# A recurrent layer's third chunk: its sa by tokens is transposed from saT instead of computed as a product of its own

## The chip, the cores and the metric

The kernel runs on one core of a Trainium2 chip. The metric is device time in microseconds of one execution. Before the change three runs took 644.02, 644.89 and 645.16 us, a median of 644.89 us.

## What is computed

A recurrent attention block (RWKV-7 style) feeds a feed-forward block with an exact GELU. All arrays are float32 in the recurrence; batch 4, 8 heads, 768 tokens, head dimension 40. For the feed-forward block the 3072 tokens have 320 features each, and 2048 hidden units.

```python
for t in range(S):
    y[:, :, t] = np.einsum('bhd,bhde->bhe', rt, state)
    Sa = np.einsum('bhde,bhe->bhd', state, at)
    state_decay = state * wt[:, :, None, :] - np.einsum('bhd,bhe->bhde', Sa, bt)
    state = state_decay + np.einsum('bhd,bhe->bhde', vt, kt)
...
x = np.ascontiguousarray(attn_out.transpose(0, 2, 1, 3)).reshape(B * S, H * D)
h = x @ w_in
g = 0.5 * h * (1.0 + erf(h * inv_sqrt2))
return (g @ w_out).astype(np.float32)
```

## The kernel before

**Chunks.** The 768 tokens are cut into 12 chunks of 64 (c = 0 to 11). Within a chunk the recurrence is turned into matrix products: masked token-by-token matrices N, A, M and RV, the inverse of a triangular matrix (Tt, built by an elimination on GpSimd), and the products that give the chunk's outputs and the state for the next chunk. Four batches times eight heads make 32 small problems, which sit two by two on the partition halves of TensorE, so that one such product is 32 matmuls of 64x64 or 64x40. A float32 matmul is shown in the trace as two matmuls and two weight loads.

**The feed-forward part** of a chunk (`ph`: the first matrix, `gelu`, `po`: the second) is laid between the steps of the recurrence of later chunks, so that TensorE has long products to run while the other engines mask, copy and transpose.

**Order.** Nothing is scheduled by a program: every engine carries out its instructions in the order in which the kernel's functions are called. Chunks 0 to 4 stand written out call by call; from chunk 5 on a loop does it. The change lies in the written-out part, at the end of the third chunk (c = 2, lines 1864 to 1893).

**sa.** For a chunk the vectors Sa of all its tokens are needed in two layouts. `saT` (line 1064) has features on partitions; it enters M = `products(saT, rT)`. `sa` by tokens enters the state tile `SM` next to the masked M, and `make_QY` multiplies `SM` with the scaled b. There are two ways to get the second layout:

- `make_sa` and `copy_sa` (lines 1050 and 1059): a second product of the same two factors as saT with their roles exchanged, 32 matmuls of 64x40 into the PSUM tile `sap`, and one copy of 128x640 by ScalarE into `SM`. Chunks 0 to 2 do this.
- `sa_blocks` (line 1082): `turn_sa` lets VectorE transpose `saT` in 32x32 blocks into a tile `sa` (it takes the place named "nT" in SBUF), and `move_sa` copies 16 blocks to where they belong in `SM`: blocks 0 to 3 by VectorE (32x256), 4 to 7 by ScalarE (32x256), and 8 to 15 by ScalarE (32x64). Chunks 3 and 4 use it; later chunks call the two halves of it apart.

**PSUM places.** PSUM is used as four places of two banks; the table `places` (line 99) says by name and chunk which place a tile gets. A new tile in a place waits until the last reader of the old one is done. In the stretch of the change: M_ps of chunk 2 is in place 2, sap of chunk 2 in place 1, kT_ps of chunk 3 in place 2, the `ph` tile that follows in place 1, A_ps of chunk 3 in place 2.

**Fills.** `keep(n)` asks for a filler matmul of n times 128 columns; the next call of `duo` (line 125), whatever tile that is for, issues it into that tile ahead of the tile's own products.

**Side tiles.** `saT` and the `vT` of the next chunk share one place in SBUF ("late"), so `turn_v(3)` waits until all readers of saT are done. The raw pairs of r of the next chunk are loaded by SyncE (`load_r(4)`) once `turn_r(3)` has read the old ones.

Of the kernel before, what the change touches and what calls it, by code (L numbers as in the profile page):

```python
# [21 lines left out]
def kernel(  # L22
# [72 lines left out]
    def keep(*columns):  # L95

        asked[:] = columns
# [27 lines left out]
    def duo(name, at):  # L125
        pt = psum.tile([P, 2, 512], FP32, tag="duo" + places[name][at], name=name, bufs=1)
        while asked:
            n = asked.pop()
            mm(pt[:, 0, :n * P], ident, cum_m.unsqueeze(1).to_broadcast([P, n, P]))
        return pt  # L130

    def half(j, n=HP):
        return slice(j * HP, j * HP + n)
# [4 lines left out]
    def mm(o, lhsT, rhs, first=True):  # L138
        nc.tensor.matmul(o, lhsT, rhs, start=first, stop=True, skip_group_check=True)  # L139
# [204 lines left out]
    def flat(t):  # L344
        return t.rearrange("p j g n t -> p (j g n) t")
# [333 lines left out]
    def flip_k(c):  # L679
        turned_in[c]["kT_ps"] = flip(by_pair(turned_in[c]["ks"]), "kT_ps", c)  # L680
# [73 lines left out]
    def masked(to, pt):  # L754
        nc.vector.tensor_tensor(to, pt, upper.unsqueeze(1).to_broadcast([P, 2 * G * NP, C]), ALU.mult)
# [12 lines left out]
    def units():  # L768
        for i in range(NP):
            for g in range(G):  # L770
                for x in range(2):
                    for e in range(2):
                        yield g, i, x, e, i // NA, 2 * (i % NA) + x
# [276 lines left out]
    def make_sa(c):  # L1050
        t = turned_in[c]
        xs = t["xs"]
        Tt = t["Tt"]
        sap = t["sap"] = duo("sap", c)[:, :, :G * NP * D].rearrange("p x (g q a d) -> p x g q a d", g=G, q=2, a=NA)
        for g, i, x, e, q, m in units():
            at = (g * NP + i) * D
            mm(sap[half(e), x, g, q, i % NA], Tt[half(e ^ x), x, g, i], xs[half(e ^ x), x, at:at + D])

    def copy_sa(c):
        sap = turned_in[c].pop("sap")  # L1060
        copy = nc.scalar.copy if 0 < c < NS else nc.vector.tensor_copy
        copy(SM.rearrange("p g q (a x) c -> p x (g q a) c", x=2)[:, :, :, :D], sap.rearrange("p x g q a d -> p x (g q a) d"))
# [19 lines left out]
    def sa_blocks(c, blocks):  # L1082

        if "sa" not in turned_in[c]:
            turn_sa(c)
        move_sa(c, blocks)

    def turn_sa(c):
        t = turned_in[c]
        if True:  # L1090
            t["sa"] = side("sa", "nT", 1).rearrange("p g n t -> p (g n) t")
            nc.vector.transpose(t["sa"].rearrange("p n t -> p (n t)"), t["saT"].rearrange("p q m e t -> p (q m e t)"))  # L1092

    def move_sa(c, blocks):
        t = turned_in[c]
        for n in blocks:
            d, g, e, z = n // 8, n // 4 % 2, n // 2 % 2, n % 2
            to, at = e * HP + z * BL, g * HP + d * BL
            end = (BL, D)[d]
            copy = nc.scalar.copy if d or n >= 4 else nc.vector.tensor_copy  # L1100
            copy(SM[to:to + BL, g].rearrange("p q m c -> p (q m) c")[:, :, d * BL:end],  # L1101
                 t["sa"][at:at + BL, :, to:to + end - d * BL])
# [5 lines left out]
    def mask_M(c):  # L1108
        t = turned_in[c]
        masked(flat(SM)[:, :, D:], t.pop("M_ps"))  # L1110
# [316 lines left out]
    def put(c, g):  # L1427
        os = work.tile([P, DM], FP32, tag=f"os{g}", name="os")
        nc.vector.tensor_copy(os, pos[c][:, g])
        for e in range(2):  # L1430
            row = (G * e + g) * S + c * C
            nc.sync.dma_start(out=out[row:row + C], in_=os[half(e)])
# [443 lines left out]
    make_M(2)  # L1876
    put(0, 1)
    mask_M(2)
    keep(2)
    make_sa(2)  # L1880
    copy_sa(2)
    flip_k(3)
    turn_v(3)
    copy_k(3)
# [432 lines left out]
```

## Time and profile before

| | |
|---|---|
| median of three runs | 644.89 us |
| the profiled execution, its time | 643.49 us |
| its span in the profile | 641.8 us |
| TensorE matmuls, busy | 624.2 us, 14788 records |
| TensorE weight loads, busy | 553.9 us, 14788 records |
| VectorE, busy | 450.5 us |
| ScalarE, busy | 373.5 us |
| GpSimd, busy | 392.2 us |

How to read the lines below. Times are microseconds from the span's start. A line of a timeline has the start, the length, the engine (PE is TensorE's matmuls, PEld its weight loads, DVE VectorE, ACT ScalarE, POOL GpSimd, SPq the queue of SyncE), the line of the kernel, the operation, the tile written and the tiles read, the shape and the number of instructions put together; in brackets stands how long the engine had been idle before it and what it waited for. A line of the windows view has the stretch, its length, and for PE, PEld, DVE, ACT and POOL the busy time with the number of instructions in brackets; then TensorE's granted clock, the DMA engines' share and GB/s. A line of the chain has start, length and what ran; "issue" is time in which the engine waited for nothing that the profile shows. A line of a DMA queue has packets, MB and the time of the packets as a share of 16 engines' span.

### The profile page before, as it was taken

How to read it: one execution, taken by the hardware profiler on the slowest of the kernel's cores; microseconds unless marked ns; L12 is line 12 of the kernel's file. 1: busy time of each engine (PE TensorE's matmuls, PEld its weight loads, DVE VectorE, ACT ScalarE, POOL GpSimd, SP SyncE). 2: the span in 40 equal slices, each digit the busy share in tenths (PEclk: the TensorE clock that was granted, in tenths of full speed). 3: DMA queues.
4: the chain of work that ended last, by engine and by line, in shares of the span. 5: the costliest groups of instructions: out<-in, count | busy, mean ns of one | idle time of the engine just before them, and what ended most of it. 6: DMA issues, size and time to landing. Idle time of an engine off the chain costs nothing.

```text
span 641.8 us, 32951 instructions
## 1 busy us (share of the span) xinstructions
PE 624.2 (97%) x14788; PEld 553.9 (86%) x14788; DVE 450.5 (70%) x604; ACT 373.5 (58%) x717; POOL 392.2 (61%) x806
## 2 busy tenths in 40 slices
PE   6899899999999999999999999999999999999997
PEld 4787788787878899998998998988989989989977
DVE  1775889996467899685995995985987965623313
ACT  4437694664265479447487587576587687274020
POOL 7587478822857814898848858858758768620000
PEclk9999899999999999999999999999999999999999
DMA  9986767448234643465555466374465450210100
GB/s 139 176 143 138 131 137 164 104 106 149 60 75 75 117 99 67 94 113 120 111 105 100 95 116 115 74 130 86 80 120 106 84 98 5 43 25 10 35 2 21
DMA packets 227119, 60.47 MB, mean 94 GB/s; under 512 B 208603, under 2 KB 225275, under 8 KB 226978
## 3 DMA queue, kind: packets, MB, share of 16 engines
q1 hardware_dynamic: 225946, 56.33, 47.2%
q8 instruction: 116, 1.90, 1.3%
q0 software_dynamic: 592, 1.70, 1.2%
q10 hardware_dynamic: 440, 0.33, 0.2%
q14 instruction: 25, 0.20, 0.1%
HBM read 50.46 MB, written 3.93 MB: 85 GB/s over the span
## 4 chain that ended last, share of the span: by engine, by line
PE 86%; DVE 4%; POOL 3%; SPq 2%; DMA 2%; ACT 2%; issue 1%; ACTq 0%; DVEq 0%; POOLq 0%
PE ph L1414 33%; PE po L1317 22%; PE QY L139 7%; PE po L1424 5%; PE po L1250 2%; PE J L139 2%; PE N_ps L139 2%; PE RV_ps L139 2%; PE saT_ps L139 2%; PE M_ps L139 2%; POOL st L863 2%; POOL st L861 2%; PE A_ps L139 1%; PE X L139 1%; PE av L139 1%
## 5 line engine op out<-in xcount | busy, mean ns | idle before, releaser
L1414 PE MATMUL ph<-xt,w_in_sb 64*64 64x256 f32 (+1 forms) x3360 | 218.4, 377 | 1.9 <-issue 1.8
L1414 PEld LDWEIGHTS ph<-xt,w_in_sb 64*64 64x64 f32 (+1 forms) x3360 | 175.1, 141 | 30.1 <-DMA v_pairs<-in_v_dram 1.7
L861 POOL TENSOR_TENSOR tmp<-W,Nb 128x126 f32<-128x126 f32 (+22 forms) x310 | 129.5, 418 | 57.6 <-DVE Nb L876 34.1
L863 POOL TENSOR_TENSOR W<-W,tmp 128x126 f32<-128x126 f32 (+22 forms) x310 | 147.3, 475 | 24.3
L1418 ACT ACTIVATE gt<-ph 128x1024 f32<-128x1024 f32 x48 | 49.2, 1025 | 92.4 <-PE ph L1414 89.0
L1317 PE MATMUL po<-w_out_sb,gt 128*128 128x160 f32 x576 | 84.3, 302 | 0.0
L1317 PEld LDWEIGHTS po<-w_out_sb,gt 128*128 128x128 f32 x576 | 79.2, 190 | 1.2
L1218 ACT COPY turned<-within 8x64 f32<-8x64 f32 (+3 forms) x144 | 46.4, 322 | 3.5 <-DVE within L1207 1.6
L814 POOL TENSOR_TENSOR VR<-VR,upper 128x1024 f32<-128x1024 f32 x8 | 18.9, 2366 | 30.2 <-ACT VR L810 26.7
L580 ACT COPY part<-part 32x256 f32<-32x256 f32 (+1 forms) x112 | 36.1, 322 | 1.7
L1424 PE MATMUL po<-w_out_sb,gt 128*128 128x320 f32 x128 | 36.5, 438 | 0.5 <-DVE w_out_sb L386 0.5
L1092 DVE STREAM_TRANSPOSE sa<-saT 128x1024 f32<-128x1024 f32 x9 | 11.1, 1238 | 32.1 <-ACT saT L1079 32.1
L1101 ACT COPY SM<-sa 32x64 f32<-32x64 f32 (+1 forms) x108 | 31.8, 294 | 1.4
L1424 PEld LDWEIGHTS po<-w_out_sb,gt 128*128 128x128 f32 x128 | 23.7, 190 | 10.2 <-DVE w_out_sb L386 1.0
L1340 DVE TENSOR_TENSOR os<-os,po 128x160 f32<-128x160 f32 x63 | 19.7, 314 | 17.4 <-PE po L1317 10.5
L1337 ACT COPY os<-po 128x160 f32<-128x160 f32 x9 | 2.6, 290 | 41.9 <-PE po L1317 41.9
L376 ACT ACTIVATE conv<-conv,rebias 128x320 uint32<-128x320 uint32 (+1 forms) x26 | 15.8, 620 | 15.7 <-DVE conv L373 15.6
L1317 PE MATMUL po<-extra,half 128*128 128x160 f32 x160 | 23.2, 299 | 0.0
L876 DVE STREAM_TRANSPOSE Nb<-N 128x1024 f32<-128x1024 f32 x10 | 21.6, 2158 | 1.7 <-ACT N L798 1.7
L1035 DVE COPY Tt<-J 32x512 f32<-32x512 f32 x9 | 6.2, 689 | 23.2 <-PE J L139 23.2
L1317 PEld LDWEIGHTS po<-extra,half 128*128 128x128 f32 x160 | 22.2, 190 | 0.0
L1317 PE MATMUL po<-extra,gt 128*128 128x160 f32 x144 | 21.1, 300 | 0.0
(301 smaller groups left out, 1280.7 us busy)
## 6 DMA issues: line engine op xcount, KB each, us to landing
VR<-in_v_dram SPq DMA_DIRECT2D x24, 160.0 KB
out_dram<-os SPq DMA_DIRECT2D x45, 80.0 KB
b_rows<-in_b_dram SPq DMA_DIRECT2D x22, 160.0 KB
k_rows<-in_k_dram SPq DMA_DIRECT2D x22, 160.0 KB
a_pairs<-in_a_dram SPq DMA_DIRECT2D x18, 144.0 KB
v_pairs<-in_v_dram SPq DMA_DIRECT2D x36, 72.0 KB
r_pairs<-in_r_dram SPq DMA_DIRECT2D x36, 72.0 KB
a_pairs<-in_b_dram SPq DMA_DIRECT2D x16, 144.0 KB
```

The lines of the kernel that those rows point to most:

```text
L139: nc.tensor.matmul(o, lhsT, rhs, start=first, stop=True, skip_group_check=True)
L580: nc.scalar.copy(to[at:at + BL, :, x, z * BL:end], tmp[on:on + BL, e, :, q * BL:q * BL + end - z * BL])
L861: eng.tensor_tensor(t, W[:, :rows, j:j + 1].to_broadcast([P, rows, rest]), Nb[:, j:j + 1, j + 1:].to_broadcast([P, rows, rest]), ALU.mult)
L863: eng.tensor_tensor(W[:, :rows, j + 1:], W[:, :rows, j + 1:], t, ALU.add)
L876: nc.vector.transpose(Nb.rearrange("p s t -> p t s"), N[:, :, :BL].rearrange("p n t -> p t n").unsqueeze(2).to_broadcast([P, BL, 2, NBL]))
L1101: copy(SM[to:to + BL, g].rearrange("p q m c -> p (q m) c")[:, :, d * BL:end], t["sa"][at:at + BL, :, to:to + end - d * BL])
L1218: nc.scalar.copy(tn[to:to + deep, :, at:at + wide], within[0][at:at + deep, :, to:to + wide])
L1317: nc.tensor.matmul(self.pt[at][:, n, :DM // 2], l_[:, f], r_[:, f], start=f == 0, stop=f == NF // 2 - 1)
L1340: nc.vector.tensor_tensor(to, one_, other, ALU.add)
L1414: nc.tensor.matmul(pt[to:end, x, s], w_in_sb[half(x), kt, p * P + to:p * P + end], xt[half(x), kt], start=kt == 0, stop=kt == NK - 1)
L1418: nc.scalar.activation(gt[:, 4 * q:4 * q + 4].rearrange("p (x s) t -> p x s t", x=2), phs.pop((c, q)), ACT.Gelu)
L1424: nc.tensor.matmul(pos[c][:, g], gt[:, f, g * P:(g + 1) * P], w_out_sb[:, f], start=f == 0, stop=f == NF - 1)
```

## The change

In the third chunk `sa` by tokens is taken from saT: `sa_blocks(2, ...)` takes the place of `make_sa(2)` and `copy_sa(2)`.

```diff
     make_M(2)
     put(0, 1)
     mask_M(2)
+    sa_blocks(2, range(0, 8))
     keep(2)
-    make_sa(2)
-    copy_sa(2)
+    sa_blocks(2, range(8, 16))
     flip_k(3)
     turn_v(3)
     copy_k(3)
```

On each engine:

- TensorE: the 32 matmuls of `sap` are removed (64 matmuls and 64 weight loads in the trace). The filler of 256 columns that `keep(2)` asks for stands ahead of kT_ps of chunk 3, where it stood ahead of `sap`.
- VectorE: one transpose of 128x1024 and four copies of 32x256 stand between the mask of M and the transposes of v and r of chunk 3.
- ScalarE: four copies of 32x256 and eight of 32x64 stand where the copy of `sap` stood, ahead of the copy of kT_ps.
- GpSimd and SyncE: the same instructions in the same order.

## The prediction

> **What bounds the kernel now.** I read the page first: busy shares, the chain that ended last, the queues.
>
> ```profile
> span 641.8 us, 32951 instructions
> PE 624.2 (97%) x14788; PEld 553.9 (86%) x14788; DVE 450.5 (70%) x604; ACT 373.5 (58%) x717; POOL 392.2 (61%) x806
> ...
> q8 instruction: 116, 1.90, 1.3%
> ...
> PE 86%; DVE 4%; POOL 3%; SPq 2%; DMA 2%; ACT 2%; issue 1%; ACTq 0%; DVEq 0%; POOLq 0%
> ```
>
> TensorE is busy for 97% of the span and holds 86% of the chain, so a microsecond more or less in TensorE's stream is a microsecond of the kernel unless it falls where TensorE waits for somebody. So I went to TensorE's own order in time around the change (start, length, engine, line, operation):
>
> ```profile
> 160.95 1.11 PE L139 MATMUL M_ps<-rT,saT 40*64 40x64 f32 x64
> 162.00 0.70 PE L139 MATMUL sap<-cum_m,ident 128*128 128x256 f32 x2
> 162.62 1.14 PE L139 MATMUL sap<-avs,Tt 64*64 64x40 f32 x64
> 163.70 1.09 PE L587 MATMUL kT_ps<-ident,extra 128*128 128x128 f32 x8
> 164.72 4.59 PE L1414 MATMUL ph<-xt,w_in_sb 64*128 64x256 f32 x40
> ```
>
> There is no idle time here: every piece starts before the one above it has drained. Third come VectorE and ScalarE in the same stretch:
>
> ```profile
> 162.13 1.22 DVE L755 TENSOR_TENSOR SM<-M_ps,upper 128x1024 f32<-128x1024 f32 x1 [1.60 <-PE M_ps L139]
> 163.28 1.24 DVE L217 STREAM_TRANSPOSE vT<-v_pairs 128x1024 f32<-128x1024 f32 x1
> 164.43 1.20 DVE L217 STREAM_TRANSPOSE rT<-r_pairs 128x1024 f32<-128x1024 f32 x1
> ```
>
> ```profile
> 164.83 1.01 ACT L685 COPY kT<-kT_ps 128x1024 f32<-128x1024 f32 x1 [0.30 <-PE kT_ps L587]
> ```
>
> **The change, part by part.** *The product.* make_sa(2) goes: 64 matmul records, issued from 162.62 until kT_ps follows at 163.70, so 1.08 us. Its copy on ScalarE goes too; it ran under the MLP's ph and was worth nothing to TensorE.
>
> *The fill.* It is not gone. keep(2) asks for it and the next PSUM tile gets it; that was sap and is now kT_ps. So 162.62 - 162.00 = 0.62 us stay, in front of kT_ps.
>
> *A new wait.* kT_ps lies in PSUM place 2, and so does M_ps of this chunk. The fill writes kT_ps, so it waits until VectorE's mask has read M_ps. Until now the product, in place 1, ran under that mask. M_ps drains at 162.06, the mask starts at 162.13 and ends at 163.35; with the same 0.07 back to TensorE, the fill starts at 163.42 instead of 162.00. Behind it stand kT_ps and ph, and nothing else in TensorE's order can go first. Stream: 1.42 later, 1.08 shorter, **+0.34 us**. Bounds: the mask frees its place when the next VectorE operation starts (163.28), +0.20; or the restart costs 0.3 more, +0.64. So this edit alone is a small loss in place of a gain.
>
> *The transpose and the copies.* Prices come from the fourth chunk, which already does this:
>
> ```profile
> 207.28 1.22 DVE L1092 STREAM_TRANSPOSE sa<-saT 128x1024 f32<-128x1024 f32 x1
> 208.54 1.74 DVE L1101 COPY SM<-sa 32x256 f32<-32x256 f32 x4
> ```
>
> ```profile
> 209.51 1.62 ACT L1101 COPY SM<-sa 32x256 f32<-32x256 f32 x4
> 213.96 2.05 ACT L1101 COPY SM<-sa 32x64 f32<-32x64 f32 x8
> ```
>
> VectorE transposes where vT stood, 163.28 to 164.50. ScalarE is idle then and copies until 164.55 + 1.62 + 2.05 = 168.2; copy_k(3) is queued behind and ends at 169.25 (+1.01). A_ps waits for it, and shares its place. The cover is ph, now 165.06 to 169.6: 0.35 us to spare, cost nothing. Without that cover A_ps is late by whatever the copies overrun. QY, which reads SM, and the mask of A, which reuses sa's place, both come after A_ps, past 168.2. VectorE's four copies end at 166.25, so vT and rT end at about 168.6 instead of 165.6; VectorE's next work is the mask of A.
>
> One step moves with rT: SyncE's eight loads of the next r pairs wait for it.
>
> ```profile
> 165.66 3.78 SPq L209 DMA_DIRECT2D r_pairs<-in_r_dram  x8
> ```
>
> ```profile
> 195.97 1.24 DVE L217 STREAM_TRANSPOSE rT<-r_pairs 128x1024 f32<-128x1024 f32 x1
> ```
>
> They would issue from 168.7 to 172.5 and are read at 195.97: no cost. GpSimd's list is unchanged.
>
> *The instruction stream itself.* The chain has two pieces in which TensorE waited for nothing that the profile shows:
>
> ```profile
> 219.47 0.33 issue
> ...
> 429.40 1.47 issue
> ```
>
> The queue named "instruction" moves 1.90 MB in 116 packets, 16.4 KB each; TensorE alone has 2 x 14788 = 29576 matmuls and weight loads, 255 to a packet. So these packets are TensorE's program, 256 instructions of 64 bytes each. Are the idle pieces packets that came late? Counts of the windows view between the ends of three such waits (PE and PEld in x):
>
> ```profile
> 87.62:219.79 132.17, 131.35 (x2798) 108.57 (x2799) 103.38 (x158) 70.88 (x116) 86.82 (x190) 1.00 0.56 112
> 219.79:430.86 211.07, 209.60 (x5354) 195.99 (x5354) 175.84 (x217) 143.27 (x294) 146.28 (x290) 1.00 0.54 102
> ```
>
> 5597 is 21.9 packets and 10708 is 41.8; with the semaphore instructions, which the view leaves out, I take them as 22 and 42: all three waits sit on packet boundaries. The DMA view for 424.5 to 428.35 and for 428.35 to 430.87 shows how it happens:
>
> ```profile
> q1 hardware_dynamic: 3082, 0.71, 104.5%
> ```
>
> ```profile
> q8 instruction: 1, 0.02, 2.8%
> ```
>
> In the first stretch data fills the DMA engines and no instruction packet moves; in the second one comes, and TensorE goes on at 430.87, 2.5 us after that stretch began.
>
> The change takes 64 matmuls and 64 weight loads out at 162.6, exactly half a packet. **Every later boundary falls 128 instructions further on in the program.** That matters where a packet is used up quickly. Counting on from 219.80 in steps of 256, shifted by 128, the new packets that are used up fastest cover these stretches of the old trace (a window also counts what runs across its edges, so 256 shows as 258 to 293):
>
> ```profile
> 186.50:188.26 1.76, 1.76 (x143) 1.69 (x136) 1.76 (x3) 1.66 (x3) 0.96 (x2) 1.00 0.26 60
> 238.12:239.88 1.76, 1.76 (x144) 1.72 (x142) 1.76 (x2) 1.06 (x3) 0.00 (x0) 1.00 1.05 223
> 255.96:258.31 2.35, 2.35 (x142) 2.32 (x136) 2.35 (x4) 2.25 (x7) 2.04 (x5) 1.00 0.87 183
> 263.31:265.69 2.38, 2.38 (x138) 2.38 (x132) 0.79 (x2) 0.00 (x0) 1.99 (x6) 1.00 0.21 34
> 288.31:290.69 2.38, 2.38 (x128) 2.22 (x130) 2.31 (x6) 2.33 (x5) 2.38 (x2) 1.00 0.30 61
> 305.63:307.64 2.01, 2.01 (x136) 2.01 (x132) 1.97 (x5) 1.77 (x4) 1.70 (x5) 1.00 0.67 130
> 380.75:382.94 2.19, 2.19 (x140) 1.97 (x141) 2.19 (x4) 2.07 (x4) 0.38 (x1) 1.00 1.16 197
> 535.75:537.95 2.19, 2.19 (x133) 2.17 (x127) 1.66 (x4) 1.46 (x3) 1.80 (x6) 1.00 0.04 7
> 580.75:582.63 1.88, 1.88 (x135) 1.88 (x130) 0.00 (x0) 1.64 (x3) 0.00 (x0) 1.00 0.03 9
> ```
>
> They are pairs of 128-instruction products back to back (J and X, QY and M, N and J). Two of the old packets for comparison: the one used up fastest, which does not idle, and the one that runs dry at 429.40 (256 instructions back from 430.87 is 426.27):
>
> ```profile
> 334.82:336.74 1.91, 1.91 (x134) 1.74 (x133) 1.91 (x3) 1.87 (x4) 0.46 (x1) 1.00 0.89 153
> 426.26:429.40 3.13, 3.13 (x153) 2.46 (x140) 3.13 (x5) 2.97 (x6) 1.24 (x4) 1.00 0.98 161
> ```
>
> What a packet needs bounds the cost. If 1.91 us is always enough, the nine cost 0.15 + 0.15 + 0.03 = 0.3. The second ran dry after 3.13 us; if that is the need, they cost 9 x 3.13 - 18.90 = 9.3. I take 2.5, the row at 430.87, nearest because it times a packet until its first instruction: 0.74 + 0.74 + 0.15 + 0.12 + 0.12 + 0.49 + 0.31 + 0.31 + 0.62 = **+3.6 us**. The two old waits (1.80) leave their places; the new boundaries meet the same bursts of data, so I put as much back: 0, bounds -1.8 and +1.8.
>
> The Trainium skill (Runtime: NRT & Kernel Launch, Instruction fetch mechanics) says that the sequencer takes its instructions in blocks of 256, fetching the next while the present one runs, mostly hidden because dispatch is slower than the refill. This trace agrees on the block and differs on the hiding, by 1.47 us in one place; by the rule the sum would be the +0.34 alone.
>
> **Sum:** 0.34 + 3.6 + 0 = +3.9 us. The profiled execution took 643.49 (1.7 around its span), so 647.4 on its account. It lies below all three timed runs; on their median of 644.89 the sum gives **648.8**, which I predict.
>
> **Rivals.**
> *The local sum alone.* Packets wait no more than now: +0.34, 645.2. For it: the old packet of 1.91 us passes without idling. Against it: new ones of 1.76, one of them under a DMA share of 1.05.
> *Faster.* The boundaries leave the two places where they idle, and no new place runs dry: 0.34 - 1.80 = -1.5, 643.4. It decides if a packet needs at most about 1.8 us. For it: only three blocks are shorter than 1.91. Against it: some fifty further fetches would all have to miss bursts of data like the one before 428.35.
> *ScalarE late.* If each of the twelve copies takes the 0.435 of VectorE's, kT is ready at 164.55 + 5.2 + 1.0 = 170.8 and A_ps slips by 1.2: alone 646.4, on top of the forecast 650.0. Against it: ScalarE's own rows say 3.67.
> *The change does not shorten TensorE's list by 128*, because waits are added as instructions: a shift of a few does not move the boundaries back, so this costs the same.
>
> **How the numbers follow.** Forecast 0.72, ScalarE late 0.06, local alone 0.15, faster 0.07. The forecast's own range is 646 to 652. Below 644.8 lie the faster case and part of the local one; upwards a need of 2.9 us (9 x 2.9 - 18.90 = 7.2) gives 652.4. Range 644.8 to 652.4. A measurement tells about 0.2%, 1.3 us, from no change: slower 0.78, same 0.15, faster 0.07.
>
> **What would show it.** TensorE idle by about 1.4 us before the fill of kT_ps, put down to VectorE's mask: the local sum. The pieces "issue" of the chain growing from 1.8 us after 200 to several, in J, X, QY, M and N: the packets. No wait of A_ps for ScalarE. It would be wrong if "issue" stays under 2 us, or if a new wait for DMA or ScalarE turns up in a later chunk.

## The result, and the profile after

| | before | after |
|---|---|---|
| median | 644.45 us (4 runs, 641.05 to 645.16) | 652.66 us (4 runs, 649.84 to 653.12) |
| ratio | | 1.014, 95% interval 1.0107 to 1.0172 |
| profiled execution: time, span | 643.49, 641.8 us | 652.90, 651.2 us |

The change costs 8.2 us by the medians, and the interval of the ratio lies clear of 1. The page of the changed kernel:

```profile
span 651.2 us, 32839 instructions
...
PE 627.0 (96%) x14724; PEld 551.1 (85%) x14724; DVE 453.9 (70%) x609; ACT 376.1 (58%) x728; POOL 388.4 (60%) x806
...
q8 instruction: 115, 1.88, 1.3%
...
PE 85%; SPq 4%; POOL 3%; issue 3%; DMA 2%; DVE 1%; ACT 1%; DVEq 0%; POOLq 0%; ACTq 0%
```

The list of TensorE is 64 matmuls and 64 weight loads shorter, and yet its busy time grew by 2.8 us and "issue" in the chain went from 1% to 3%. (That share also counts pieces ahead of the change and of other engines; TensorE's own waits after 162 us that are put down to "issue" went from 1.8 to 5.1 us.) So look first at the stretch of the change (TensorE's timeline), where the loss might be expected:

```profile
162.23 1.11 PE L139 MATMUL M_ps<-rT,saT 40*64 40x64 f32 x64
164.69 0.70 PE L139 MATMUL kT_ps<-cum_m,ident 128*128 128x256 f32 x2 [1.35 <-DVE SM L755]
165.22 1.04 PE L587 MATMUL kT_ps<-ident,extra 128*128 128x128 f32 x8
166.19 4.59 PE L1414 MATMUL ph<-xt,w_in_sb 64*128 64x256 f32 x40
170.71 1.16 PE L139 MATMUL A_ps<-aT,kT 40*64 40x64 f32 x64
```

The idling before the fill is there, 1.35 us put down to VectorE's mask. From M_ps to ph it is now 3.96 us; it was 3.77. The local loss is 0.19 us. ScalarE and SyncE in the same stretch:

```profile
165.82 3.67 ACT L1101 COPY SM<-sa 32x256 f32<-32x256 f32 x12 [3.87 <-DVE sa L1092]
169.52 1.02 ACT L685 COPY kT<-kT_ps 128x1024 f32<-128x1024 f32 x1
```

```profile
170.00 4.47 SPq L209 DMA_DIRECT2D r_pairs<-in_r_dram  x8
```

kT is copied by 170.54, A_ps begins at 170.71 right behind ph: nothing waits. The 9.4 us between the two spans therefore part in three: M_ps begins 1.28 us later than in the other execution (the program up to there is the same; that is one execution against another), 0.19 us in the stretch, and 7.93 us after ph has begun. Where those are lost the chain shows; first the kernel before, then the changed one, at the same instructions of the fourth chunk:

```profile
187.03 0.93 PE N_ps L139 x64
187.97 0.68 PE J L139 x50
188.65 4.50 PE po L1424 x16
```

```profile
188.77 0.93 PE N_ps L139 x64
189.70 0.50 PE J L139 x39
190.20 1.70 issue
191.90 0.38 PE J L139 x21
192.28 6.20 PE po L1424 x16
```

In the middle of the product J TensorE stands still for 1.70 us and waits for nothing that has a name. The product po behind it takes 6.20 us instead of 4.50. The windows view says why (the third number from the end is the granted clock); first the kernel before, then the changed one:

```profile
188.60:191.00 2.40, 2.40 (x15) 1.77 (x10) 0.92 (x1) 2.35 (x5) 0.00 (x0) 1.00 0.16 25
191.00:193.20 2.20, 2.20 (x11) 1.55 (x9) 2.00 (x1) 2.08 (x9) 0.00 (x0) 1.00 1.03 204
```

```profile
192.30:195.40 3.10, 3.10 (x8) 2.08 (x9) 2.13 (x1) 2.89 (x10) 0.21 (x1) 0.65 0.39 81
195.40:198.50 3.10, 3.10 (x11) 2.07 (x10) 0.00 (x0) 0.00 (x0) 2.40 (x10) 0.80 0.00 0
```

After the idling the clock is granted at 0.65 and 0.80, where the kernel before had 1.00. Further on the chain has more such pieces, in QY, ahead of ph and ahead of A_ps:

```profile
222.19 0.73 issue
...
272.93 0.74 issue
...
324.45 0.61 issue
```

TensorE's instructions can also be set against each other one by one, by when they start in the two executions, leaving out the 128 that are gone. The difference rises by about 0.2 us or more, and stays up, at fourteen places. From the first that follows the change on, every rise stands at a multiple of 256 instructions from the one after "190.20 1.70 issue", and nearly every fall (the waits of the kernel before that have vanished) half a packet from there; counted in matmuls and weight loads, the distance falls short of an exact multiple by about one instruction per packet, and the records leave the semaphore instructions out. The changes, by the time of the instruction in the kernel before:

```
up:    173.4 +0.3   188.3 +1.9   216.6 +1.0   239.9 +0.6   258.3 +0.7   265.7 +1.0   307.7 +0.7
       315.5 +0.8   382.9 +0.4   454.1 +0.2   477.1 +1.0   498.6 +0.3   545.8 +0.4   582.6 +0.5
clock: 188.7 to 193.2 (po) +1.7
down:  219.8 -0.6   314.5 -0.2   336.7 -0.3   430.9 -1.9   435.0 -0.4   500.1 -0.3   523.6 -0.2
```

### The profile page after: what moved, and what is told of

Same layout as the page of the kernel before. It is cut to its first block, busy times and chain, and to the rows that moved or that the text cites. A ratio compares the mean times of both kernels' runs of the same rounds, so it can differ in the third digit from the quotient of the medians.

```text
span 651.2 us, 32839 instructions
## 1 busy us (share of the span) xinstructions
PE 627.0 (96%) x14724; PEld 551.1 (85%) x14724; DVE 453.9 (70%) x609; ACT 376.1 (58%) x728; POOL 388.4 (60%) x806
## 4 chain that ended last, share of the span: by engine, by line
PE 85%; SPq 4%; POOL 3%; issue 3%; DMA 2%; DVE 1%; ACT 1%; DVEq 0%; POOLq 0%; ACTq 0%
PE ph L1414 30%; PE po L1317 19%; PE QY L139 7%; PE po L1424 6%; PE J L139 3%; PE po L1250 2%; PE M_ps L139 2%; PE sq L139 2%; PE A_ps L139 2%; SPq L194 2%; PE RV_ps L139 2%; PE N_ps L139 2%; PE saT_ps L139 2%; PE av L139 2%; POOL W L863 2%
## 5 line engine op out<-in xcount | busy, mean ns | idle before, releaser
L1414 PEld LDWEIGHTS ph<-xt,w_in_sb 64*64 64x64 f32 (+1 forms) x3360 | 171.2, 141 | 34.7 <-issue 4.5
L863 POOL TENSOR_TENSOR W<-W,tmp 128x126 f32<-128x126 f32 (+22 forms) x310 | 143.0, 461 | 24.3
L1101 ACT COPY SM<-sa 32x64 f32<-32x64 f32 (+1 forms) x120 | 35.3, 294 | 5.4 <-DVE sa L1092 3.9
L1424 PE MATMUL po<-w_out_sb,gt 128*128 128x320 f32 x128 | 37.9, 453 | 0.0
L848 POOL MEMSET W<- 128x512 f32 x10 | 5.3, 526 | 35.0 <-ACT T L908 20.7
```

What stands on the lines that cost most here:

```text
L863: eng.tensor_tensor(W[:, :rows, j + 1:], W[:, :rows, j + 1:], t, ALU.add)
L1414: nc.tensor.matmul(pt[to:end, x, s], w_in_sb[half(x), kt, p * P + to:p * P + end], xt[half(x), kt], start=kt == 0, stop=kt == NK - 1)
L1424: nc.tensor.matmul(pos[c][:, g], gt[:, f, g * P:(g + 1) * P], w_out_sb[:, f], start=f == 0, stop=f == NF - 1)
```

## The experiments

Three theories were put against each other: the loss is where the 256-instruction packets of TensorE's program begin; it is the transpose, the copies and what they push back; it is the wait of kT_ps for the mask. Since single executions differ by some microseconds ahead of the change, each profile is also read from the start of the ph that follows kT_ps to the end of the span; there the kernel before takes 641.8 - 164.72 = 477.08 us.

| kernel | packet boundaries after the change, moved by | median | ratio to before, 95% | ph to end, us | against before |
|---|---|---|---|---|---|
| changed | 128 | 652.66 | 1.014 (1.0107 to 1.0172) | 651.2 - 166.19 = 485.01 | +7.93 |
| e1, product kept | 0 | 646.87 | 1.0012 (0.999 to 1.0034) | 643.7 - 166.10 = 477.60 | +0.52 |
| e2, product twice | 128 | 652.64 | 1.0114 (1.0088 to 1.014) | 650.6 - 168.17 = 482.43 | +5.35 |
| e3, product thrice | 256 | 647.66 | 1.0048 (1.0027 to 1.0068) | 646.4 - 168.89 = 477.51 | +0.43 |
| e4, half the product | 64 | 648.01 | 1.0029 (0.9995 to 1.0064) | 648.7 - 169.14 = 479.56 | +2.48 |
| e5, other PSUM places | 128 | 652.13 | 1.0111 (1.0062 to 1.016) | 650.1 - 167.90 = 482.20 | +5.12 |
| e7, shift at the start | 128 | 664.96 | 1.0311 (1.0259 to 1.0363) | 663.3 - 178.85 = 484.45 | +7.37 |
| e8, change and shift | 0 (128 ahead of it) | 658.11 | 1.0201 (1.0119 to 1.0282) | 654.8 - 177.11 = 477.69 | +0.61 |

The last column sorts by the second: 0.4 to 0.6 us where the boundaries lie on the old instructions, 2.5 a quarter of a packet away, 5.1 to 7.9 half a packet away. It rests on one execution of each kernel. Two entries hold a wait of A_ps for ScalarE besides, 0.28 us in e4 and 1.22 in e5.

**e1: the change, with the product back in TensorE's list.**

```diff
     sa_blocks(2, range(0, 8))
     keep(2)
+    make_sa(2)
     sa_blocks(2, range(8, 16))
```

> The changed kernel with the product and its fill put back (32 matmuls into sap, which nothing reads): TensorE's list is that of the kernel before, VectorE and ScalarE do all that the change gives them. Packet theory (the loss is where the 256-instruction packets of TensorE's program begin): 643.5 to 646.5, ratio to before 0.998 to 1.004, and the pieces 'issue' after 200 us under 3 us. Rival A (the loss comes from the transpose, the twelve copies and what they push back on VectorE, ScalarE and SyncE): 650 to 653, ratio 1.010 or more. Rival B (the wait of kT_ps for the mask and what it pushes back): near before as well, since the product covers the mask again; this run does not part it from the packet theory.

The ratio is 1.0012, not to be told from before. VectorE and ScalarE do all the new work here, so that work is not the loss. Its chain has two longer pieces "issue" that the chain of the kernel before has not, 0.64 us in QY at 173.79 and 0.44 at 501.50, both at boundaries of the kernel before. The product J runs through (chain of e1):

```profile
190.23 0.68 PE J L139 x51
190.91 4.50 PE po L1424 x16
```

and a wait of the kernel before is back at its old place, after 25 records of ph:

```profile
429.56 1.51 PE ph L1414 x25
431.08 1.22 issue
```

**e2: the kernel before, with the product issued twice.**

```diff
-        for g, i, x, e, q, m in units():
+        for _ in range(2 if c == 2 else 1):
+            for g, i, x, e, q, m in units():
```

> The kernel before with the third chunk's product issued twice into the same tile: no transpose, no block copies, no wait for the mask, and 128 instructions more, so every later packet boundary lies half a packet from where it was, as in the changed kernel. Packet theory: +1.1 for the product and +7 to +8 of waits, 652 to 655, ratio 1.011 to 1.017. Rivals A and B: +1.1 alone, 645 to 647, ratio 1.001 to 1.003.

The ratio, 1.0114, is at the lower edge of what the packet theory expected: 5.35 us from ph on, where +7 to +8 of waits had been said. Nothing of the change is in this kernel but the half packet, and that was added, not removed. Its chain has the wait at the same point of J (39 records in), and the windows view the low clock behind it:

```profile
191.91 1.39 issue
```

```profile
193.40:197.00 3.60, 3.60 (x28) 2.47 (x29) 2.11 (x1) 3.46 (x11) 0.09 (x1) 0.53 0.66 130
```

This run also parts the packets from the wait for the mask, which e1 could not: e2 has no such wait.

**e3: the product three times** (range(3) in the same line).

> The kernel before with the same product issued three times: 256 instructions more, a whole packet, so later boundaries lie on the old instructions again. Packet theory: +2.2 alone, 645.5 to 648.5, ratio 1.001 to 1.006, less than the run with 128 more. If more instructions as such cost the time, it comes out above that run: 655 to 662, ratio 1.018 or more.

1.0048, about 3.1 us, of which two more products are 2.2; a boundary now falls into these products themselves, with 0.69 us of "issue" at 166.12. It has more instructions than e2 and is 5 us quicker. With a whole packet more, 0.43 us are left from ph on; that many instructions as such cost little beyond their own time.

**e4: the change, with half of the product.**

```diff
-        for g, i, x, e, q, m in units():
+        for g, i, x, e, q, m in (islice(units(), 16) if c == 2 else units()):
```

It has the call of make_sa(2) from e1, and issues 16 matmuls of it.

> The changed kernel with half of the product put back (16 matmuls, 64 instructions) and the fill ahead of it: boundaries lie a quarter of a packet from the old ones. Packet theory: between, 646 to 650.5, ratio 1.003 to 1.010; the two waits at old boundaries gone, others in their place, all on boundaries moved by 64. Rival A: 650 to 653. Rival B: the wait for the mask is half covered, so about half of the loss, 648 to 649.

The ratio, 1.0029, lies at the lower edge of what was expected, and its interval reaches down to no loss. By the profile 2.48 us are lost from ph on, under a third of the changed kernel's. The rival that blames the wait for the mask had 648 to 649 here, and 648.01 came: this run does not part it from the packets, e2 and e5 do.

**e5: the change, without the wait for the mask.**

```diff
-        ("kT_ps", "1232"),
-        ("A_ps", "111223331111"),
+        ("kT_ps", "1231"),
+        ("A_ps", "111123331111"),
...
-        ("ph", "333223122310132303000300010001000100010001001302"),
+        ("ph", "333223222310132303000300010001000100010001001302"),
```

> The changed kernel with kT_ps of the fourth chunk in PSUM place 1, the ph tile that follows in place 2 and A_ps in place 1, so that the fill and kT_ps need not wait for the mask of M. Same instructions, same packet boundaries. Packet theory: the 1.35 us of idling before the fill goes, the rest of the loss stays: 650.5 to 653, ratio 1.008 to 1.014. Rival B (the wait for the mask and what it pushes back is the loss): back to 645 or less, ratio under 1.002.

The time stays (1.0111). The timeline of TensorE shows that the wait has gone and another has come:

```profile
165.36 1.11 PE L139 MATMUL M_ps<-rT,saT 40*64 40x64 f32 x64
166.40 0.70 PE L139 MATMUL kT_ps<-cum_m,ident 128*128 128x256 f32 x2
...
173.71 1.16 PE L139 MATMUL A_ps<-aT,kT 40*64 40x64 f32 x64 [1.22 <-ACT kT L685]
```

The fill follows M_ps at once, ph starts 1.42 us sooner after M_ps, and so A_ps now has to wait 1.22 us for ScalarE, whose twelve copies have not moved. Here the mask's wait could not be won back alone: the copies are the next limit. The boundaries' loss is still there: the chain has "issue" at the same instruction of J as the changed kernel, 1.67 us at 193.30. "ScalarE late" was a rival of the prediction; it is false for the change and true for this kernel.

**e6: what a packet needs, by itself.** Ahead of the last chunk's feed-forward part, where little data is moved:

```diff
+    pt = duo("warm", 0)
+    for n in range(192):
+        for q in range(2):
+            mm(pt[lo[q], 0, :BL], ident[lo[q], lo[q]], ident[lo[q], lo[q]])
     run(mlp(NCH - 1))
```

> The kernel before with 384 matmuls of 32x32 put ahead of the last chunk's feed-forward part, where hardly any data is moved: 1536 instructions, six packets, used up one after the other. It measures what a packet needs by itself. Packet theory: TensorE runs in bursts with an idle piece at each packet boundary, 3.5 to 4.2 us from packet to packet, 20 to 25 us in all. If TensorE's own pace sets it, about 8 us (the J product's 128 instructions take 0.7), with no idle pieces.

One execution, 667.28 us. The timeline:

```profile
607.55 4.30 PE L139 MATMUL warm<-ident 32*32 32x32 f32 x260 [0.41 <-DVE os L1340]
613.18 14.75 PE L139 MATMUL warm<-ident 32*32 32x32 f32 x508 [1.33 <-issue]
```

It took 20.3 us, at the lower edge. The first two packets (260 matmuls and as many weight loads) run at 2.1 us each without a pause; then TensorE idles 1.33 us. The other 508, four packets, take 14.75: **3.7 us from packet to packet**. Long idle pieces between these had been expected; they do not appear, since the clock had fallen and TensorE itself needed nearly as long:

```profile
611.90:613.20 1.30, 0.02 (x2) 0.01 (x2) 0.00 (x0) 0.00 (x0) 0.00 (x0) 0.92 0.00 0
613.20:615.00 1.80, 1.80 (x69) 1.80 (x70) 0.00 (x0) 0.00 (x0) 0.00 (x0) 0.50 0.04 9
```

The starts of the instructions still show a pause of 0.35 us at each boundary, 3.75 us apart, so the packets, and not TensorE, set this pace.

The trace's records of the queue "instruction" say more. At these three pauses a packet starts to move 1.1 to 1.5 us after TensorE has passed the boundary before, moves for 0.9 to 1.1 us, and TensorE goes on 1.3 to 1.5 us later. For the wait in J of the changed kernel the three pieces are 0.9, 1.3 and 1.45 us. And in none of the ten profiled executions do two packets of TensorE's program start less than 3.34 us apart, with much data moving or with little. So one packet is under way at a time, and 256 instructions that are used up in less than that live on what has been fetched ahead.

**e7: the kernel before, 32 small matmuls more at its very start.**

```diff
     for n in range(3):
         mm(pt[:, n % 2], w_in_sb[:, 0, :P], w_in_sb[:, 0, :512])
+    for n in range(16):
+        for q in range(2):
+            mm(pt[lo[q], 0, :BL], w_in_sb[lo[q], 0, :BL], w_in_sb[lo[q], 0, :BL])
```

> The kernel before with 32 matmuls of 32x32 added to the three that warm TensorE up at the very start, where TensorE then waits for data anyway: all packet boundaries of the whole kernel move by half a packet, and nothing else changes. Packet theory: 651 to 660, ratio 1.009 to 1.024, with idle pieces that begin where those of the changed kernel do after 162 us. Every theory that blames the third chunk's work: 645 to 646, ratio under 1.002.

The loss is 3.1%, some 20 us, more than expected: the stretch before 160 us, for which nothing had been worked out, loses more than the rest, and its granted clock averages 0.94 against 0.99 in the kernel before. From ph on it is +7.37, next to the +7.93 of the changed kernel, and the wait in J is at the very same instruction (39 records in):

```profile
202.61 0.50 PE J L139 x39
203.11 1.43 issue
204.53 0.38 PE J L139 x21
```

**e8: the change, with the same 32 matmuls at the start.**

> The changed kernel with the same 32 matmuls at the start: boundaries ahead of the change move by half a packet, those behind it lie where they lay in the kernel before. Packet theory: the waits after 162 us are those of the kernel before (the one at J after 190 us and the low clock behind it gone), the time is lost ahead of 162 us instead: 646 to 652, below the changed kernel and below the run with the shift alone. If only the change's own work counts: 652 to 653, as the changed kernel.

The sum came out wrong, 658.11, above the changed kernel, because the part ahead of the change loses as in e7. The mechanism came out as stated but for one wait: behind the change it is +0.61 us from ph on, J runs through with the clock at full behind it, and the chain after 160 us has two pieces "issue" of more than 0.1 us, one in QY, where the kernel before has none (e1 has 0.64 there), and the old one of ph:

```profile
184.74 1.05 issue
...
442.74 0.93 issue
```

No kernel that beats the one before came out of this. The changed kernel with the product put back for its instruction count alone (e1) equals it within the interval of 0.999 to 1.0034, and what could still be won in the stretch, about the product's 1.08 us, is less than these measurements resolve.

## Why the prediction was right and wrong

*Direction and cause: right.* The local sum was +0.34 and measured 0.19, by the steps given: the product gone, the fill kept, 1.35 us of waiting for the mask (1.42 was said). The cover of ScalarE's copies was put at 0.35 us; kT was ready 0.17 before A_ps began. The loads of r moved back without a cost. The signs that the prediction named came as well: TensorE idle ahead of the fill, "issue" after 162 us up from 1.8 to 5.1 us, no wait of A_ps for ScalarE. One new wait in a later chunk is put down to a DMA, 0.41 us ahead of ph at 485.84; that is a packet boundary too, its weight load is put down to "issue", and ph does not read the array named. That the boundaries move by half a packet, and that this outweighs the local sum, is shown by e2 and e7, which have none of the change's other parts, and by e1, e3 and e8, in which the loss behind the change goes when the boundaries are back.

*Size: wrong.* 648.8 was predicted, with an upper end of 652.4; 652.66 came. The term that failed is the +3.6 for late packets, in three ways.

First, the price. 2.5 us was taken as what a packet needs, from one place, between the clearing of the data and the packet's first instruction. That leaves out the time from the boundary until the packet starts to move: 0.9 us at J and 1.1 to 1.5 in e6. What a packet needs when several are wanted in a row is 3.7 us (e6), and no two started less than 3.34 us apart. The packet of 1.76 us at 186.5 needed 1.9 more, 3.66. With a quieter packet ahead a new one costs less; over the nine the rises above come to 1.9 + 0.6 + 0.7 + 1.0 + 0 + 0.7 + 0.4 + 0 + 0.5 = 5.8 instead of 3.6. Why packets start no closer together no run here shows.

Second, packets that last longer than 2.5 us were put at nothing. The rises at 173.4, 216.6, 315.5, 454.1, 477.1, 498.6 and 545.8 are theirs, 4.0 us; by the starts of the instructions these lasted 2.6 to 3.9 us in the kernel before.

Third, a term was missing altogether: the clock after the wait in J, po at 6.20 instead of 4.50, 1.7 us.

The term put at 0 for the old waits, with new ones in exchange, had -1.8 as its lower bound; the old ones took 3.9 us with them, and what came in their place is counted above. 5.8 + 4.0 + 1.7 - 3.9 = 7.6, next to the 7.9 from ph on; the rest is in shifts of under 0.2 us. That the time came out only 0.3 us above the range is in part luck: the terms that were missed upwards were met by old waits that vanished.

*The rivals.* "The local sum alone" is refuted by e1 and e2 together, "faster" by the result. "ScalarE late" did not happen, but waits behind the mask (e5).

## What to carry to other kernels

When TensorE is the bound and its program is long, an edit that adds or removes instructions also moves every later packet boundary; test it against a version with the same number of instructions before you credit or blame the work itself. Count how long each run of 256 instructions lasts: where two short products stand back to back, a boundary just ahead of them cost from nothing to 1.9 us at the nine places here. Compare that length with the 3.34 us that was the shortest time between two packets. A kernel whose waits named "issue" are few may owe it to where its boundaries happen to lie, so an edit that is right by itself can lose to that.

## What was not expected of the hardware

Behind a wait of 1.70 us the granted clock averaged 0.65, and behind one of 1.39 us 0.53 (e2), where small products stood around it; in e5 a wait of 1.67 at the same instruction was followed by po at 4.50, with no such loss. The records of the clock show it halved for 3.41 us in the changed kernel (from 193.25), e2 (193.39) and e7 (206.0), and its changes lie multiples of 3.41 us apart. In these three the whole wait lies within the last 3.41 us before the fall; in e5 such a step, counted on from the last change at 70.85, falls at 193.7, inside the wait from 193.30 to 194.97. That alone does not decide it: the wait of 1.47 us at 429.40 in the kernel before also lies within one step, and the clock stayed. In e6 the clock stayed at 0.50 while TensorE worked through 508 matmuls of 32x32. The Trainium skill (TensorE: Matmul & The Clock Gate, Part 1: The HAM clock gate) has the clock halved after an idle window of about 3.4 us that runs freely; that the same wait does it in one run and not in another agrees with a free-running window, while the length does not: these waits were half as long.

Of what the Trainium skill says (Runtime: NRT & Kernel Launch, Instruction fetch mechanics), the blocks of 256 instructions are borne out by e3, where a whole packet more costs little beyond the products' own 2.2 us. That crossing into a new block is mostly hidden is not: e2 loses 1.1%, the added product's own 1.1 us included, and e7 3.1%, by where the blocks begin.
